# Where the second and third expert's rows stand in the queues of an attention and expert kernel

## The chip, the cores and the metric

The kernel runs on one core of one Trainium2 chip. The metric is the device time of one execution in microseconds (us); several runs are made and their median is compared. The engines have an in-order instruction stream each: TensorE (PE; its weight loads are PEld), VectorE (DVE), ScalarE (ACT), GpSimd (POOL) and SyncE (SP, which only issues transfers here). A tile framework writes the streams: it takes the program's instructions in its order and places each in its engine's queue by its own plan of what is ready when, and it adds the semaphore waits.

## The reference

Three steps, each on the output of the one ahead. The change lies in the second.

```python
# 1. attention: B 2, H 8, S 576, head dim 64; half of the heads local, half strided masks -> x, 1152 x 512
# 2. mixture of experts: E 8, F 1024, capacity 288; one expert for a token
logits = x @ w_gate                      # 512 x 8
expert_idx = argmax(logits, 1); gate_w = softmax(logits)[expert_idx]
disp[e, place in e] = x[token]           # rows of an expert's tokens
h = maximum(disp @ w1, 0)                # 512 -> 1024
y = h @ w2                               # 1024 -> 512
out[token] = gate_w * y[e, place in e]
# 3. feed-forward: h = out @ w_in (512 -> 2048); (h - tanh(h)) @ w_out
```

## The kernel before

All products of the experts and of the feed-forward are made with float16 pairs: a float32 operand is split into a high and a low part (`split`: ScalarE writes the high part, VectorE the low part), and a product is three matmuls, high by high, high by low, low by high (`mm3`). Weights come as float32 in 1 MB halves (`load_w`, tile `st`, four buffers, issued by SyncE) and are split in pieces (`split_w`) into `w1h`, `w1l`, `w2h`, `w2l`. A fifth load into `st` waits until VectorE has split the first.

After attention and routing, the loop over the eight experts `e` runs:
- `gather(e)`: GpSimd fetches the rows of an expert's tokens by index into two tiles `xg` of 96 rows (four buffers, so two experts at a time).
- `tokens(e)`: ScalarE scales `xg` by the gates in place, TensorE transposes it (four small matmuls for a half, out of `xg` with the identity in `iw`), ScalarE and VectorE split the transposed half into `xh` and `xl`.
- `stage1(e)`: the first products, four groups (`fp` 0 to 3) of 24 matmuls of 192 columns; after each group ScalarE applies the relu and writes `hh`, VectorE writes `hl`. Ahead of each group stand some items of `extra`, the splits of weights needed later. The tokens of the next expert (`mid`) are called ahead of group 1.
- `stage2(e - 1)`: the second products of the expert ahead, 96 matmuls with `hh`, `hl` and the second weights; the result goes to `x2h`, `x2l`, in the order of the experts.

`w10`, `w11` and `w20` are loads made early, in attention: first weights of experts 0 and 1, second weights of expert 0. Before, what is left of `w11` (two pieces) and all of `w20` (four) is split in `stage1(0)`. `expert_order` and `token_ids` compute, between the stages, where a token goes; they give small VectorE operations and small products (`ob`, `oa`). `piece` splits a part of `w_in` or `w_out` (tile `raw`, three buffers). `keep_warm` runs matmuls on zeros (`zz`) while the routing is under way. `tc.issue_after(i)` makes an instruction stand behind `i` on the same engine; `behind()` does so for ScalarE and VectorE with their latest instructions.

The profile writes nearly all instructions as line 75, that of the helper that remembers an engine's last instruction; they are told apart by their tiles.

Of the kernel before, what the change touches and what calls it, by code (L numbers as in the profile page):

```python
# [21 lines left out]
E, F1 = 8, 1024  # L22
# [35 lines left out]
BETA = C0 / C2 - ALPHA * ALPHA  # L58
# h - tanh(h) by odd powers of h from the third on
SERIES = [1.0 / 3, -2.0 / 15, 17.0 / 315, -62.0 / 2835, 1382.0 / 155925, -21844.0 / 6081075, 929569.0 / 638512875,  # L60
# [4 lines left out]
class _Last:  # L65
    """An engine that remembers its last instruction."""

# [14 lines left out]
def kernel(  # L82
# [9 lines left out]
    act, dve, pool, pe = _Last(nc.scalar), _Last(nc.vector), _Last(nc.gpsimd), _Last(nc.tensor)  # L92
    sp = nc.sync

    @contextmanager
    def behind():
        # what the block adds on ACT and DVE is issued after what they have so far
        with tc.issue_after(act.last.ins), tc.issue_after(dve.last.ins):
            yield
# [9 lines left out]

# [1 line left out]
    iw = cst.tile([P, NCH, P + E], F32, name="iw")  # L111
# [15 lines left out]

# [1 line left out]
    # sums of the low parts: not finite where a high part is not  # L129
    lsum = cst.tile([P, NLS], F32, name="lsum")  # L130
    lcol = iter(range(NLS))
    pool.memset(lsum, 0.0)

    # sums of squares of a part of each operand, over their least
    sq = cst.tile([P, len(SQ_MIN)], F32, name="sq")
# [24 lines left out]
    def f64_split(hi, lo, raw, scale, n=512):  # L160
        # the bits of -w 2^128 as a float32; sizes from 1 on come out as not finite. A shift by three leaves the two
        # top bits of the exponent set; the last three bits of the fraction are the top ones of the low word
        top = raw.rearrange("p (n two) -> p n two", two=2)[:, :, 1]
        low = raw.bitcast(U16).rearrange("p (n four) -> p n four", four=4)[:, :, 1]
        a = f64p.tile([P, n], U32, tag="fa", name="fa")
        act.activation(a, low, AF.Copy, scale=2.0 ** -13, bias=2.0 ** -14 - 0.5)
        dve.scalar_tensor_tensor(a, top, 3, a, op0=ALU.logical_shift_left, op1=ALU.bitwise_or)
        dve.scalar_tensor_tensor(a, top, 0x80000000, a, op0=ALU.bitwise_and, op1=ALU.bitwise_xor)
        square_once("w_in" if scale == SWI else "w_out", hi, a.bitcast(F32), 2.0 ** -128)
        split(hi, lo, a.bitcast(F32), -scale * 2.0 ** -128, check=True)  # L170
# [26 lines left out]
    def get_w(w, e, n=2):  # L197
        # the halves, and what splits them bit by bit
        lds = [load_w(w, half, e) for half in range(2)]
        return [ld[1:3] for ld in lds], [lambda ld=ld, i=i: split_w(ld, i, n) for ld in lds for i in range(0, NCH, n)]  # L200
# [20 lines left out]

# [1 line left out]
    KT = STRIDE + S + 64  # L223
# [5 lines left out]
    act.activation(warm, warm, AF.Exp)  # L229
    # the clock of the products' array rises while the first rows are on their way  # L230
    zz = cst.tile([P, 512], BF16, name="zz")
# [9 lines left out]
    WARM = (2, 7, 5, 6, 3, 3)  # L241
    # rows past the keys stay zero: the products take all 128 rows
    for t in vts:
# [9 lines left out]
    def load_qk(b, hp, first=False):  # L253
        qt = pa.tile([P, NST * P], F32, tag="q", name="qt")
        kt = pa.tile([P, KT], F32, tag="k", name="kt")
        if first:
            # what the first group of tiles takes goes first
            sp.dma_start(mk[:, :4 * P], masks[:, :4 * P])
# [21 lines left out]

    # the last ones are local: only their last tiles' tokens wait for the end
    pairs = [(0, 0), (0, 1), (0, 2), (0, 3), (1, 2), (1, 3), (1, 0), (1, 1)]
# [82 lines left out]
    def logits_part(first, c, xT, parts, late):  # L365
        # parts: (tile of tokens, where it starts in the sequence)
        lp = bank()
        lv = lp[:, : len(parts) * (P + E)].rearrange("p (t e) -> p t e", e=P + E)
        xw = pa.tile([P, 3, P], F32, tag="xw", name="xw", bufs=4)
        for i, (t, s0) in enumerate(parts):  # L370
            r0, r1 = max(0, -s0), min(P, S - s0)
            pe.matmul(lv[r0:r1, i, :], xT[:, s0 + r0:s0 + r1], iw[:, c, :], start=True, stop=True)
        # whole tiles in one go, a part of a tile by itself
        whole = [k for k, (t, s0) in enumerate(parts) if 0 <= s0 <= S - P]
# [33 lines left out]
    def last_logits(xT, tl, t0):  # L408
        # the routing waits for these: straight onto the other pairs' sums, and the rows of x after them
        c = pairs[-1][1]  # L410
# [31 lines left out]

# [1 line left out]
    def bce(ap, n):  # L444
# [17 lines left out]
    def route(a, b, src):  # L462
        # tokens' experts, ranks and slots; the tiles up to b, after those up to a
        n, ts = b - a, slice(a, b)
# [4 lines left out]
        dve.tensor_tensor(oh[:, ts], bct(desc, n), bce(pm[:, ts], E), op=ALU.is_equal)  # L469
        # ranks in the bank's columns up to 72, tokens of slots in those up to 88, their gates in those past them  # L470
        if a == 0:
# [14 lines left out]
        dve.scalar_tensor_tensor(as_[:, ts], pm[:, ts], -2.0, hf[:, ts], op0=ALU.mult, op1=ALU.add)  # L486
        # the segments' numbers less 2 E, against -2 (E - e) + half
        dve.tensor_tensor(oha[:, ts], bct(seg, n), bce(as_[:, ts], NSEG), op=ALU.is_equal)
# [5 lines left out]
    def gates(a, b):  # L494
        # a slot's gate: the softmax's largest entry, in three exact parts, zero past the capacity
        n, ts = b - a, slice(a, b)
# [84 lines left out]
    def expert_order():  # L581
        # where a token goes in the order of experts, and which token a place there is
        dve.tensor_tensor(lt, bct(desc, NTT), bce(pm, E), op=ALU.is_lt)
# [37 lines left out]

# [1 line left out]
    ffr, ffn = ExitStack(), ExitStack()  # L623
# [9 lines left out]
    def gather(e):  # L633
        # the rows of an expert's tokens
        rows = []
# [7 lines left out]
    def tokens(e, rows):  # L643
        # columns of tokens times their gates
        xh = pm_.tile([P, NCH, SLOT], F16, tag="xh", name="xh")
# [20 lines left out]

    def stage1(xh, xl, whl, extra, mid=None):
        hh = pm_.tile([P, NF1, SLOT], F16, tag="hh", name="hh")
        hl = pm_.tile([P, NF1, SLOT], F16, tag="hl", name="hl")
        for fp in range(NF1 // 2):  # L670
            with behind():
                for x in extra[fp::NF1 // 2]:
                    x()
            if fp == 1 and mid:
                mid()
            hp_ = bank()
            for j in range(2):
# [4 lines left out]
                for c in range(NCH):  # L682
                    mm3(o, wh[:, c, fs], wl[:, c, fs], xh[:, c, :], xl[:, c, :], c == 0, c == NCH - 1)
            hv = hp_[:, : 2 * SLOT].rearrange("p (f k) -> p f k", f=2)
            act.activation(hh[:, 2 * fp:2 * fp + 2, :], hv, AF.Relu)
            dve.scalar_tensor_tensor(hl[:, 2 * fp:2 * fp + 2, :], hv, 0.0, hh[:, 2 * fp:2 * fp + 2, :],
                                     op0=ALU.max, op1=ALU.subtract)
# [20 lines left out]
    with behind(), tc.issue_after(last_x):  # L708
        NB = 6
# [4 lines left out]
    first_gather.append(pool.last.ins)  # L714
    xs[0] = tokens(0, rows)
    rows = gather(1)
    with tc.issue_after(pool.last.ins):
# [7 lines left out]
    for e in range(E):  # L725
        if e > 0:
            w2s[e], ex = get_w(2, e)
            if e == 1:
                for ld in wdma[-2:]:
                    after_gather(ld)  # L730
        else:
            ex = [lambda i=i: split_w(w11[i // 4], i % 4, 1) for i in range(NB, 8)]
            ex += [lambda i=i: split_w(w20[i // 2], i % 2 * 2, 2) for i in range(4)]
            k = -(-len(ex) // 4)
            ex = [ex[j * k + i] if j * k + i < len(ex) else (lambda: None) for i in range(k) for j in range(4)]

        def next_tokens():
            xs[e + 1] = tokens(e + 1, rows)

        hs[e] = stage1(*xs.pop(e), w1s.pop(e), ex, next_tokens if e + 1 < E else None)  # L740
        ex = []
# [27 lines left out]
    ffr.close()  # L769
# [1 line left out]
    pw = ffn.enter_context(tc.tile_pool(name="pw", bufs=1, reuse_waits="tile"))  # L771
# [31 lines left out]
    def ffn2(k, gh, gl):  # L803
# [12 lines left out]
        if k == 0:  # L816
            # the later weights are still on their way: all tokens for a slice of them
            ops = [bank() for _ in range(nj)]
# [12 lines left out]
    def trouble():  # L831
        # on how many partitions what the way above rests on fails: the tokens of an expert fit, the series holds,
        # nothing is past float16's range, and h and a part of each operand are large enough for it
        ok = pw.tile([P, 3 + len(SQ_MIN)], F32, name="ok")
# [20 lines left out]
    def general():  # L855
        # any counts and sizes: all experts for all tokens in float32, weighted by the gate or zero
        with ExitStack() as gx:
# [68 lines left out]
    def tanh_shrink(pool_, hp):  # L926
        # a series up to h^2 = 1/4, past it the difference
        def t(name):
# [34 lines left out]
def _layout(inputs):  # L963
# [6 lines left out]
    a = {}  # L970
    # local heads: pairs of heads; 64 queries against 96 keys
    ql = np.zeros((B, 2, 2, D, NLT, 2, 64), dt)
# [34 lines left out]
    a["w_out"] = np.ascontiguousarray(inputs["moe2_w_out"]).view(np.uint64)  # L1007
    # constants of the shapes alone
    NEG = -1.0e10
# [47 lines left out]
```

## Time and profile before

| | us |
|---|---|
| runs of the kernel before | 434.90, 431.78, 432.42 |
| median of these | 432.42 |
| span of the profiled execution, first to last instruction | 432.6 |
| TensorE busy | 399.6 |
| VectorE busy | 298.4 |
| ScalarE busy | 261.6 |
| GpSimd busy | 39.3 |

The profiled execution is one execution; its own time is not listed beside its span, which lies within the runs' range. Experts run from about 96 to 240 us of the span, the feed-forward from there to the end. Matmuls are pipelined: the starts of two matmuls in a row tell what one costs, the duration written beside it is longer. A granted clock of 1.0 is 2.4 GHz, of 0.5 is 1.2 GHz.

### The profile page before, as it was taken

What the parts mean: (1) busy time and instruction counts of PE and PEld (TensorE: products, weight loads), DVE (VectorE), ACT (ScalarE), POOL (GpSimd) and SP (SyncE); (2) the same over time, 40 slices, a digit from 0 to 9 for tenths busy, and PEclk for the clock granted to TensorE, in tenths of its full rate; (3) what the DMA queues carried; (4) which work ended last, traced back from release to release, by engine and by line L of the source; (5) the groups of instructions that cost most, each with busy time, mean ns of one, the idle gap of its engine ahead of it and who ended that gap; (6) DMA issues with size and microseconds to landing.
All of it is one profiled execution on the core that took longest, in us unless ns stands there. A gap on an engine that the chain in (4) does not pass through costs nothing.

```text
span 432.6 us, 8410 instructions
## 1 busy us (share of the span) xinstructions
PE 399.6 (92%) x3192; PEld 298.5 (69%) x3192; DVE 298.4 (69%) x752; ACT 261.6 (60%) x612; POOL 39.3 (9%) x44
## 2 busy tenths in 40 slices
PE   6699598864999999999999999999999999999994
PEld 3598598723999999999999566665444655444441
DVE  2388589772898979899999799999983678000000
ACT  3377387443996777876974799899752887100000
POOL 6000000066102011000000000000000100000000
PEclk9699699995999999999999999999999999999998
DMA  8797488626879788789724423312350100000000
GB/s 217 218 295 230 152 269 236 213 93 205 291 262 354 279 291 302 243 302 341 259 101 148 147 97 113 131 59 89 99 194 17 58 1 2 24 27 27 24 26 27
DMA packets 33514, 69.92 MB, mean 162 GB/s; under 512 B 3108, under 2 KB 9252, under 8 KB 33468
## 3 DMA queue, kind: packets, MB, share of 16 engines
q1 hardware_dynamic: 31580, 63.68, 44.7%
q0 software_dynamic: 1744, 5.51, 3.8%
q8 instruction: 27, 0.44, 0.4%
q14 instruction: 19, 0.16, 0.1%
q10 hardware_dynamic: 144, 0.13, 0.1%
HBM read 64.59 MB, written 4.72 MB: 160 GB/s over the span
## 4 chain that ended last, share of the span: by engine, by line
PE 42%; DVE 9%; issue 8%; DMA 3%; ACT 2%; POOL 0%; POOLq 0%; DVEq 0%; ACTq 0%
PE bank L75 42%; DVE w2l L75 3%; DMA xg<-xd,ids 2%; DVE w1l L75 2%; DVE fa L75 2%; DVE hl L75 1%; ACT w2h L75 1%; DMA out_dram<-ob,ids 1%; ACT win_h L75 1%; DVE x2l L75 0%; DVE xl L75 0%; DVE win_l L75 0%; ACT x2h L75 0%; POOL xg L75 0%; POOL out_dram L75 0%
## 5 line engine op out<-in xcount | busy, mean ns | idle before, releaser
L75 PE MATMUL bank<-xh,w1h 128*128 128x192 f16 x256 | 64.0, 250 | 7.6 <-ACT xh L75 7.6
L75 PE MATMUL bank<-xh,w1l 128*128 128x192 f16 x256 | 64.1, 250 | 0.7 <-DVE w1l L75 0.5
L75 PE MATMUL bank<-xl,w1h 128*128 128x192 f16 x256 | 64.0, 250 | 0.0
L75 PE MATMUL bank<-x2l,win_h 128*128 128x384 f16 x192 | 62.6, 326 | 0.5 <-DVE ok L75 0.5
L75 PE MATMUL bank<-hl,w2h 128*128 128x192 f16 x256 | 63.0, 246 | 0.0
L75 PE MATMUL bank<-hh,w2h 128*128 128x192 f16 x256 | 63.0, 246 | 0.0
L75 PE MATMUL bank<-hh,w2l 128*128 128x192 f16 x256 | 63.0, 246 | 0.0
L75 PE MATMUL bank<-x2h,win_h 128*128 128x384 f16 x192 | 62.6, 326 | 0.0
L75 PE MATMUL bank<-x2h,win_l 128*128 128x384 f16 x192 | 62.6, 326 | 0.0
L75 PEld LDWEIGHTS <-win_h 128*128 128x128 f16 x384 | 37.6, 98 | 25.8 <-DVE ok L75 0.7
L75 PE MATMUL bank<-wo_h,gh 128*128 128x512 f16 x144 | 54.6, 379 | 0.0
L75 PE MATMUL bank<-wo_l,gh 128*128 128x512 f16 x144 | 54.6, 379 | 0.0
L75 PE MATMUL bank<-wo_h,gl 128*128 128x512 f16 x144 | 54.6, 379 | 0.0
L75 PEld LDWEIGHTS <-gh 128*128 128x128 f16 x288 | 28.1, 98 | 33.6
L75 PEld LDWEIGHTS <-w1h 128*128 128x128 f16 x512 | 47.2, 100 | 0.3
L75 PEld LDWEIGHTS <-w2h 128*128 128x128 f16 x512 | 46.1, 98 | 0.0
L75 DVE SCALAR_TENSOR_TENSOR fa<-raw,fa 128x512 uint32<-128x512 uint32 x64 | 42.8, 684 | 2.1 <-ACT fa L75 1.7
L75 ACT ACTIVATE ob<-bank 128x512 f32<-128x512 f32 x9 | 5.4, 597 | 62.6 <-PE bank L75 60.1
L75 DVE SCALAR_TENSOR_TENSOR w2l<-st,w2h 128x1024 f16<-128x1024 f32 x32 | 38.8, 1217 | 2.9 <-ACT w2h L75 2.6
L75 DVE SCALAR_TENSOR_TENSOR w1l<-st,w1h 128x1024 f16<-128x1024 f32 (+1 forms) x40 | 38.4, 1003 | 0.3 <-ACT w1h L75 0.2
L75 DVE SCALAR_TENSOR_TENSOR w<-z,y 128x384 f32<-128x384 f32 x48 | 26.0, 552 | 15.2 <-ACT z L75 15.2
L75 PE MATMUL bank<-kt,qt 128*108 128x108 f32 (+2 forms) x160 | 23.5, 292 | 12.1 <-DMA kt<-in_k_str_dram 5.7
(144 smaller groups left out, 765.5 us busy)
## 6 DMA issues: line engine op xcount, KB each, us to landing
st<-in_w_dram SPq DMA_DIRECT2D x32, 1024.0 KB, 5.8
raw<-in_w_in_dram SPq DMA_DIRECT2D x16, 512.0 KB, 5.6
raw<-in_w_out_dram SPq DMA_DIRECT2D x16, 512.0 KB, 3.5
qt<-in_q_str_dram SPq DMA_DIRECT2D x4, 594.0 KB, 6.0
xd<-xw SPq DMA_DIRECT2D x15, 128.0 KB, 2.0
vt<-in_v_loc_dram SPq DMA_DIRECT2D x4, 432.0 KB, 6.1
qt<-in_q_loc_dram SPq DMA_DIRECT2D x3, 576.0 KB, 9.0
kt<-in_k_str_dram SPq DMA_DIRECT2D x4, 297.0 KB, 6.7
```

Source lines behind the costliest of these rows:

```text
L75: self.last = f(*a, **k)
```

## The change

The tokens of expert 1 are called ahead of group 3 of `stage1(0)` instead of group 1, those of expert 2 ahead of group 2 of `stage1(1)` (`mid_at` is 3 - e for the first two experts, else 1). Their instructions stand behind the matmuls so far on TensorE, and on ScalarE behind the relu of group 1 (for expert 1) or group 0 (for expert 2). The splits of `w20` move from `stage1(0)` to `stage1(1)`, where they share the eight places with the splits of expert 1's own second weights; of the two pieces left of `w11` both come ahead of group 0. Comments also go, which only moves line numbers.

```diff
-    def stage1(xh, xl, whl, extra, mid=None):
+    def stage1(xh, xl, whl, extra, mid=None, mid_at=1):
...
-            if fp == 1 and mid:
-                mid()
+            if fp == mid_at and mid:
+                with tc.issue_after(pe.last.ins) if fp > 1 else nullcontext():
+                    mid()
...
             act.activation(hh[:, 2 * fp:2 * fp + 2, :], hv, AF.Relu)
+            relus[fp] = act.last.ins
...
             if e == 1:
+                ex = w20s[::2] + ex[::2] + w20s[1::2] + ex[1::2]
                 for ld in wdma[-2:]:
                     after_gather(ld)
         else:
-            ex = [lambda i=i: split_w(w11[i // 4], i % 4, 1) for i in range(NB, 8)]
-            ex += [lambda i=i: split_w(w20[i // 2], i % 2 * 2, 2) for i in range(4)]
-            k = -(-len(ex) // 4)
-            ex = [ex[j * k + i] if j * k + i < len(ex) else (lambda: None) for i in range(k) for j in range(4)]
+
+            left = [lambda i=i: split_w(w11[i // 4], i % 4, 1) for i in range(NB, 8)]
+            w20s = [lambda i=i: split_w(w20[i // 2], i % 2 * 2, 2) for i in range(4)]
+            none = lambda: None
+            ex = [left[0], none, none, none, left[1]]
 
         def next_tokens():
-            xs[e + 1] = tokens(e + 1, rows)
-
-        hs[e] = stage1(*xs.pop(e), w1s.pop(e), ex, next_tokens if e + 1 < E else None)
+
+            with tc.issue_after(relus[1 - e]) if e < 2 else nullcontext():
+                xs[e + 1] = tokens(e + 1, rows)
+
+        hs[e] = stage1(*xs.pop(e), w1s.pop(e), ex, next_tokens if e + 1 < E else None, 3 - e if e < 2 else 1)
```

ScalarE, from the scaling of expert 0's rows on (`xg<-xg,gsl`: two for each expert), before:

```order
L75 ACTIVATE xg<-xg,gsl 96x512 [waits DMASW0_49,DVE_49]
L75 ACTIVATE xg<-xg,gsl 96x512 [waits DMAHW5_49,DMAHW6_49,DMAHW4_49,DMASW1_49]
L75 ACTIVATE xh<-bank 128x4x96 [waits PE_49]
L75 ACTIVATE xg<-xg,gsl 96x512 [waits DMAHW7_49,DMASW2_49]
L75 ACTIVATE xh<-bank 128x4x96 [waits PE_49]
L75 ACTIVATE w1h<-st 128x512 x2
L75 ACTIVATE xh,sq<-bank 128x4x96 [waits PE_49]
```

The same place after the change:

```order
L75 ACTIVATE xg<-xg,gsl 96x512 [waits DMASW0_49,DVE_49]
L75 ACTIVATE xg<-xg,gsl 96x512 [waits DMAHW5_49,DMAHW6_49,DMAHW4_49,DMASW1_49]
L75 ACTIVATE xh<-bank 128x4x96 [waits PE_49] x2
L75 ACTIVATE w1h<-st 128x512 x2
L75 ACTIVATE hh<-bank 128x384 [waits PE_49] x2
L75 ACTIVATE xg<-xg,gsl 96x512 [waits DMAHW7_49,DMASW2_49]
L75 ACTIVATE xg<-xg,gsl 96x512 [waits DMAHW0_49,DMASW3_49]
```

The first scaling of expert 1 stood between the two `xh` of expert 0; now both scalings of expert 1 stand behind two relus of expert 0.

ScalarE in the groups of expert 0 and 1, before, from expert 0's first relu on (`xg` rows: experts 2 and 3):

```order
L75 ACTIVATE hh<-bank 128x384 [waits PE_49]
L75 ACTIVATE w2h,sq<-st 128x512
L75 ACTIVATE w2h<-st 128x1024
L75 ACTIVATE w2h<-st 128x1024 [waits Activation_49]
L75 ACTIVATE xh<-bank 128x4x96 [waits PE_49]
L75 ACTIVATE hh<-bank 128x384 [waits PE_49]
L75 ACTIVATE w2h<-st 128x1024 x2
L75 ACTIVATE hh<-bank 128x384 [waits PE_49]
L75 ACTIVATE xg<-xg,gsl 96x512 [waits DMASW4_49]
L75 ACTIVATE xg<-xg,gsl 96x512 [waits DMASW5_49]
```

After, from the relu of expert 0's last group on to the scalings of expert 2:

```order
L75 ACTIVATE hh<-bank 128x384 [waits PE_49]
L75 ACTIVATE w2h,sq<-st 128x512
L75 ACTIVATE w2h<-st 128x1024 [waits Activation_49]
L75 ACTIVATE w2h<-st 128x1024
L75 ACTIVATE hh<-bank 128x384 [waits PE_49]
L75 ACTIVATE w2h<-st 128x1024 x2
L75 ACTIVATE hh<-bank 128x384 [waits PE_49]
L75 ACTIVATE w2h<-st 128x1024 [waits DMAHW1_49]
L75 ACTIVATE w2h<-st 128x1024
L75 ACTIVATE xg<-xg,gsl 96x512 [waits DMASW4_49]
L75 ACTIVATE xg<-xg,gsl 96x512 [waits DMASW5_49]
```

Six `w2h` and a square now stand between expert 0's last relu and the scalings of expert 2. Right behind them, after the change, the scalings of experts 3 and 4 follow, ahead of the relu of expert 1's third group:

```order
L75 ACTIVATE xg<-xg,gsl 96x512 [waits DMASW6_49]
L75 ACTIVATE xh<-bank 128x4x96 [waits DVE_49,PE_49]
L75 ACTIVATE xg<-xg,gsl 96x512 [waits DMASW7_49]
L75 ACTIVATE xh<-bank 128x4x96 [waits PE_49]
L75 ACTIVATE xg<-xg,gsl 96x512 [waits DMASW0_49,Activation_49]
L75 ACTIVATE xg<-xg,gsl 96x512 [waits DMASW1_49,Activation_49]
L75 ACTIVATE hh<-bank 128x384 [waits PE_49]
L75 ACTIVATE w2h<-st 128x1024 [waits DMAHW3_49]
```

The last two `xg` rows are expert 4's; before, they stood behind the first `x2h` of expert 0's second products. On TensorE the eight transposes of expert 1 stood after 1 and after 24 products of expert 0 and now stand after 72; those of expert 2 stood after 24 products of expert 1 and now stand after 48. The GpSimd queue has the same rows in the same order.

## Rows read from the trace of the kernel before

**Rows 1.** Stage table: window, length, busy (x instructions) of PE, PEld, DVE, ACT, POOL; clock, DMA share, GB/s.
```profile
148.20:164.70 16.50, 16.50 (x202) 16.50 (x201) 13.34 (x25) 11.71 (x18) 1.85 (x2) 1.00 0.77 267
```
**Rows 2.** Waits of TensorE, whole span: us in total, times, longest.
```profile
PE bank L75 <- ACT xh L75: 7.6, 1, 7.6
...
PE bank L75 <- DVE ok L75: 0.5, 1, 0.5
PE bank L75 <- DVE w1l L75: 0.5, 1, 0.5
```
**Rows 3.** ScalarE in order of time: start, us, instruction, idle before and its releaser.
```profile
94.13 0.72 ACT L75 ACTIVATE xg<-xg,gsl 96x512 f32<-96x512 f32 x1 [0.88 <-DMA xg<-xd,ids]
...
102.51 0.72 ACT L75 ACTIVATE xg<-xg,gsl 96x512 f32<-96x512 f32 x1 [7.29 <-DMA xg<-xd,ids]
103.14 0.47 ACT L75 ACTIVATE xh<-bank 128x384 f16<-128x384 f32 x1
```
**Rows 4.** TensorE in order of time, at the points that the sum uses.
```profile
47.99 1.75 PE L75 MATMUL bank<-kt,qt 128*108 128x108 f32 x8 [5.66 <-DMA kt<-in_k_str_dram]
...
95.29 0.81 PE L75 MATMUL bank<-zz 128*128 128x512 bf16 x3
103.66 0.32 PE L75 MATMUL bank<-xh,w1h 128*128 128x192 f16 x1 [7.56 <-ACT xh L75]
...
114.96 0.24 PE L75 MATMUL bank<-xh,w1h 128*128 128x192 f16 x1
...
116.94 0.83 PE L75 MATMUL bank<-iw,xg 96*128 96x96 f32 x8
...
123.78 0.24 PE L75 MATMUL bank<-hh,w2h 128*128 128x192 f16 x1
...
131.69 0.25 PE L75 MATMUL bank<-xh,w1h 128*128 128x192 f16 x1
```
**Rows 5.** Stage table by single microseconds; the third number from the end is the clock.
```profile
44.00:45.00 1.00, 0.00 (x0) 0.00 (x0) 1.00 (x5) 0.59 (x2) 0.00 (x0) 0.70 1.03 334
...
51.00:52.00 1.00, 1.00 (x10) 1.00 (x10) 0.00 (x0) 1.00 (x6) 0.00 (x0) 0.89 0.05 22
...
99.00:100.00 1.00, 0.00 (x0) 0.00 (x0) 0.00 (x0) 0.00 (x0) 1.00 (x2) 0.51 1.06 408
...
109.00:110.00 1.00, 1.00 (x13) 0.97 (x12) 0.49 (x1) 1.00 (x3) 0.29 (x1) 0.87 0.95 336
```
**Rows 6.** ScalarE in order of time, splits, a relu and two scalings.
```profile
109.33 1.99 ACT L75 ACTIVATE w2h<-st 128x1024 f16<-128x1024 f32 x2
...
113.86 0.50 ACT L75 ACTIVATE hh<-bank 128x384 f16<-128x384 f32 x1
114.23 1.34 ACT L75 ACTIVATE xg<-xg,gsl 96x512 f32<-96x512 f32 x2
```
**Rows 7.** VectorE in order of time, order sums and splits.
```profile
116.83 0.17 DVE L75 COPY off<-bank 128x16 f32<-128x16 f32 x1
...
120.29 1.22 DVE L75 SCALAR_TENSOR_TENSOR w2l<-st,w2h 128x1024 f16<-128x1024 f32 x1
...
128.86 1.21 DVE L75 SCALAR_TENSOR_TENSOR w1l<-st,w1h 128x1024 f16<-128x1024 f32 x1
```
**Rows 8.** GpSimd and SyncE in order of time, then the gathers' landing times.
```profile
96.39 0.92 POOL L75 DMA_INDIRECT xg<-xd,ids  x1 [0.30 <-PE bank L75]
...
118.19 0.91 POOL L75 DMA_INDIRECT xg<-xd,ids  x1 [7.57 <-ACT xg L75]
...
105.50 0.37 SPq L186 DMA_DIRECT2D st<-in_w_dram  x1
...
DMA to landing us min/median/max: 3.1/6.0/10.4
```
**Rows 9.** DMA queues, 97 to 99 us, then 100 to 102 (q1 SyncE, q0 GpSimd): packets, MB, share.
```profile
q1 hardware_dynamic: 332, 0.72, 99.1%
...
q0 software_dynamic: 109, 0.32, 50.0%
```

More of the change, by code (lines that the diff above doesn't have):

```diff
@@ L715 @@
     xs[0] = tokens(0, rows)
+    relus = {}
     rows = gather(1)
```

## The prediction

> **What bounds the kernel now.** I read the times by stage first. In a whole expert stage TensorE is busy for all of its 16.50 us while VectorE works 13.34 and ScalarE 11.71 [rows 1]: from the experts on, the matmul queue sets the pace. Then the waits of TensorE: after the routing there is one long one, 7.6 us before a product of expert 0, released by ScalarE's xh, and two of 0.5 us [rows 2]. So what is gained up to some point of the expert stages reaches the end, unless a supplier (ScalarE, VectorE, a gather) then comes too late.
>
> ScalarE's own rows say why it waits. It scales the second half of expert 0's rows at 94.13, and its next row is a scaling for expert 1, at 102.51, after the gather landed; only behind it comes the xh of 103.14, the second half of expert 0's columns [rows 3]. The queue is in order, so expert 0 waits for expert 1's rows. TensorE's last keep-warm product ends at 95.29 + 0.81 = 96.1, its first expert product starts at 103.66 [rows 4]. The clock's share falls to 0.51 in the microsecond from 99 and is back only in that from 109 [rows 5], so the stall also makes the first 5.5 us of work run at half clock (1.2 instead of 2.4 GHz): 7.6 + some 2.7 us, about 10.2 in all, are lost. First products of expert 1 start at 114.96, those of expert 2 at 131.69 [rows 4]. The sum follows these two points.
>
> **The change, step by step.** The profiled span is 432.6 us, 0.2 above the median of 432.42; I apply the difference of the sum to the median.
>
> Expert 0 starts on time. In the new ScalarE order nothing stands between expert 0's two scalings and its two xh. The second half's four transposes end near 95.5, xh takes 0.47 [rows 3]: 96.0, and xl follows on VectorE near 96.6. The start moves from 103.66 to 96.1, with the array still warm. A product costs 7.91 / 96 = 0.0824 us (96 second products from 123.78 to 131.69) [rows 4]. The 72 products that now precede expert 1's transposes end at 96.6 + 69 x 0.0824 = 102.3.
>
> Expert 1's rows. Their gather landed at 102.5 [rows 3]; 0.72 of scaling, the second half 0.62 behind, and four transposes each (0.83 for eight [rows 4]) end at 104.4, so TensorE waits some 1.5 us. One thing could make them later. The two VectorE splits left over for expert 1 end near 98 instead of 105.4, and these free the buffer for the 1 MB load that SyncE issued at 105.50 [rows 8]; it and two loads of w_in (0.5 MB each; in the new order a third one comes ahead of the next weights) go out near 98, while expert 1's gathers, the second of them issued at 96.39 [rows 8], are in flight. From 97 to 99 SyncE's queue moved 0.72 MB and the gathers nothing, from 100 to 102 the gathers moved 0.32 MB [rows 9]: they moved when what had been issued before them was through. If order of issue decides, the new loads stand behind the gathers and cost nothing; if SyncE's queue goes first, 2 MB at 0.36 MB/us cost 5.5 us. The rows fit the first; I take 1 us and keep 0 to 5.5. Transposes end at 105.4, 24 products later, at 107.4, expert 1 starts, against 114.96: 7.6 ahead.
>
> Expert 2's rows behind the splits. The four splits of w20 now come in the first two of expert 1's four groups of products, and two splits of its own also stand ahead of the scalings. So in ScalarE's new queue six long w2h rows and one square lie between the last relu of expert 0 and expert 2's scalings. From 107.4: relu 0.38, square 0.6, then two w2h, relu, two w2h, relu, two w2h, scaling. A w2h costs 1.99 / 2, pipelined 0.95; relu 0.37; two scalings 1.34 [rows 6]. That is 0.38 + 0.6 + 3 x 1.9 + 2 x 0.37 + 0.72 = 8.1: the first half is ready at 115.6, the second at 116.2, the transposes end at 116.8. TensorE has only 48 products, 4.0 us, until it needs them: it stands still from 111.4 to 115.6. Before, these transposes came after 24 products and ended at 117.77; 24 more products make that 119.6, so 2.8 us are left of the 7.6. This is the price of the moved splits; before, they lay in the time of expert 0, beside slow products.
>
> Clock. Two waits show what 4.2 us of standing still may do. In the 5.66 us before 47.99 the clock fell in the microsecond from 44, some 2 us in, and was back in that from 51, 3.2 us after work resumed; in the 7.56 us before 103.66 it fell 2.9 us in and came back after 5.5 us of work [rows 4, 5]. At half clock 3.2 to 5.5 us of work lose 1.6 to 2.75; if it falls only as work resumes, or not at all, less. I take 1.4, ends 0 and 2.75. The other 48 products (4.0), the small products for the tokens' places (0.24) and expert 0's 96 second products (7.9) then end at 116.8 + 12.1 + 1.4 = 130.3.
>
> VectorE must have the second weights of expert 0 by then: from 107.5 the order sums (116.83 to 120.29, 3.5 us), a low part of 0.47, four w2l of 1.14 [rows 7] and one more 0.47 end at 116.5, needed from 121 on: covered.
>
> ScalarE's next knot. In the new order the scalings of experts 3 and 4, four rows, stand ahead of the relu of expert 1's third group. Expert 4's gather takes the buffers that expert 2's transposes leave; before, GpSimd began it at 118.19, 1.25 us after those transposes began at 116.94 [rows 4, 8]. Now: 116.9 and 1.2 later, and 6.0 us to landing (median; 3.1 to 10.4) [rows 8]: 124.2 for the second half, scaled at 124.9. Until then ScalarE is stuck. Behind it stand relu, two w2h, relu, then w1h of expert 2, at 127.5; on VectorE hl, two w2l, hl, then the w1l of expert 2 (1.15 each [rows 7]): 130.15 for the first, 131.3 for the second, which TensorE needs 0.5 us into expert 2. That lets expert 2 start, in effect, at 130.8. Both paths, 130.3 and 130.8, end close together; the later one decides: 131.69 - 130.8 = 0.9 us gained. With 0 instead of 1 us at expert 1's rows, the fast landing and no loss of clock it is 131.69 - 127.9 = 3.8; with the slow ends it is negative.
>
> After that the order differs little, and VectorE has 3 us to spare per stage [rows 1], so I carry 0.9 to the end: 432.4 - 0.9 = 431.5 us. The added waits (issue_after) are order of issue on one engine and cost nothing by themselves; the GpSimd queue has the same rows in the same order.
>
> **Rivals.**
> Kept: expert 2's rows don't hold TensorE up, and most of the 10.2 us stays. For it: the stall removed is real, and TensorE has hardly any other. Against: 8.1 us of ScalarE rows against 4.0 us of products is not close. It needs ScalarE's queue to stand otherwise than the order shows; time 422 to 428.
> Neutral: the lead at expert 2 is eaten further on. The wait of 0.5 us for w1l [rows 2] shows that weights come just in time; loads, gathers, scaling, splits form a ring of their own, and if it turns no earlier, TensorE meets it two experts on. Against: VectorE's 3 us of slack and gathers that follow TensorE's transposes. Time 432 to 433.
> Slower: the gathers are held back twice, expert 1's behind the 2 MB that now start at 98, expert 4's behind the loads for expert 2. It decides from 2 us of delay at expert 1 on, since then TensorE stands still for 3.5 us there too and loses the clock a second time, or from a landing of 7 us at expert 4: 131.69 is passed by 1 to 5 us. Time 433.5 to 438. For it: the one landing of 10.4 us. Against: gathers so far moved by order of issue.
> Turns: gathers and loads share the DMA engines, so that neither the 2 MB at 98 nor any backlog holds a gather up. The 1 us falls away, expert 4's rows land nearer to the 3.1 us than to the 6.0, and TensorE's own path decides: 130.3 - 1.0 = 129.3, 2.4 us gained, 430.0; without a loss of clock 428.6. For it: landings of 3.1 us occur. Against: two microseconds with 0.72 MB in SyncE's queue and no gather packet, though the gather of 96.39 was on its way [rows 8, 9].
> The Trainium skill states this rule: "DMA: Bandwidth & Descriptors", Queues, rings and completion order, says that each DMA engine takes turns between the queues that have work, a packet at a time. On these rows the trace does not agree with it.
>
> **How the numbers follow.** Forecast (430.5 to 432) 0.40, turns (428 to 430.5) 0.22, neutral 0.14, slower 0.16, kept 0.08. About 1%, 4.3 us, is what a measurement of this kernel can tell from no change: 428.1 and 436.7. Faster by more: kept and the lower edge of turns, 0.14; slower by more: the upper part of its rival, 0.10; within 1%: 0.76. The range leaves out kept and the worst of slower: 428.0 to 434.9.
>
> **What the profile after would show.** Right: no wait before expert 0's first product, at 96.1, with the clock share at 1.0 through 110; a wait of 1 to 3 us for xg before expert 1's transposes near 102; a wait of about 4 us, released by ScalarE's xg, before expert 2's transposes near 111 to 116; a clock share of 0.5 for some microseconds behind it; ScalarE idle for the gather of expert 4 at 117 to 124; expert 2's first products at 130 to 131. Wrong: no wait near 111 (then kept), or the expert-1 wait above 4 us (then slower). If expert 2 starts near 130 but the last experts no earlier than before, it is neutral.

## The result and the profile after

The changed kernel takes 436.28 us (median of six runs, 434.77 to 439.95) against 432.28 before: ratio 1.0101, 95% interval 1.0063 to 1.0139. It is about 1% slower; I had forecast 431.5, and the time lies above the range of 428.0 to 434.9. The medians in this document are over all runs, while the ratios leave out four runs that lie more than 1.5% above the fastest of their kernel, one each of hold and tokens_only and two of gather_first, and the profiles of tokens_only and gather_first are of such runs.

The profiled execution is the longest of the six (439.95, span 438.2). Attention, which the change doesn't touch, ended 1.08 us earlier in it than in the trace of before, so I count from the end of the last keep-warm product: 95.29 + 0.81 = 96.10 before [rows 4], 94.21 + 0.81 = 95.02 after. TensorE in order of time after the change (start, us, instruction, idle before and its releaser):

```profile
94.21 0.81 PE L75 MATMUL bank<-zz 128*128 128x512 bf16 x3
94.95 0.41 PE L75 MATMUL bank<-xh,w1h 128*128 128x192 f16 x3
...
102.37 0.55 PE L75 MATMUL bank<-iw,xg 96*128 96x96 f32 x4 [0.97 <-ACT xg L75]
103.46 0.55 PE L75 MATMUL bank<-iw,xg 96*128 96x96 f32 x4 [0.55 <-ACT xg L75]
105.86 0.24 PE L75 MATMUL bank<-xh,w1h 128*128 128x192 f16 x1
...
114.37 1.29 PE L75 MATMUL bank<-iw,xg 96*128 96x96 f32 x8 [4.39 <-ACT xg L75]
...
129.78 0.26 PE L75 MATMUL bank<-xh,w1h 128*128 128x192 f16 x1 [0.49 <-ACT w1h L75]
131.59 0.26 PE L75 MATMUL bank<-xh,w1l 128*128 128x192 f16 x1 [1.47 <-DVE w1l L75]
132.73 0.34 PE L75 MATMUL bank<-xh,w1l 128*128 128x192 f16 x1 [0.48 <-DVE w1l L75]
...
244.65 0.34 PE L75 MATMUL bank<-x2h,win_h 128*128 128x384 f16 x1
```

The 7.6 us ahead of expert 0 [rows 2, 4] are gone. In their place stand 1.5 us for expert 1's rows and 4.39 for expert 2's. Expert 2 starts 34.76 us after the last keep-warm product; before it was 131.69 - 96.10 = 35.59, so at that point 0.83 us were gained. The loss comes behind it. Here are the first-product stages of experts 2 to 6, each from its first product to the first second product behind it (window, length, then busy time of PE, PEld, DVE, ACT, POOL; clock third from the end), after:

```profile
129.78:142.11 12.33, 10.38 (x104) 9.80 (x105) 11.03 (x21) 9.41 (x16) 1.84 (x2) 0.86 0.91 317
150.05:160.68 10.63, 8.95 (x107) 8.49 (x106) 9.75 (x18) 7.60 (x12) 1.94 (x2) 1.00 0.95 304
168.60:178.35 9.75, 8.93 (x107) 8.48 (x106) 8.87 (x17) 6.72 (x12) 1.94 (x2) 1.00 1.01 346
186.27:196.28 10.01, 8.93 (x107) 8.48 (x106) 9.13 (x17) 6.97 (x12) 0.00 (x0) 1.00 0.98 348
204.20:212.78 8.58, 8.58 (x106) 8.58 (x105) 7.70 (x13) 4.54 (x10) 0.00 (x0) 1.00 1.02 378
```

and the stages of experts 2, 4 and 5 before, and, in order of time, the first product of the feed-forward before:

```profile
131.69:140.28 8.59, 8.59 (x108) 8.59 (x106) 7.33 (x16) 6.20 (x11) 2.43 (x2) 1.00 0.96 352
...
164.70:173.61 8.91, 8.76 (x107) 8.54 (x106) 8.03 (x15) 5.87 (x11) 1.94 (x2) 1.00 1.03 368
181.53:190.99 9.46, 8.93 (x106) 8.48 (x105) 8.58 (x17) 6.43 (x11) 0.00 (x0) 1.00 0.99 351
```

```profile
239.36 0.34 PE L75 MATMUL bank<-x2h,win_h 128*128 128x384 f16 x1
```

A stage without a wait takes 8.58. Expert 2 lost 12.33 - 8.59 = 3.74 (2.44 of waits; the rest at half clock), expert 3 2.05, expert 4 0.84, expert 5 0.55 more than before. Less the 0.83 gained that is 6.35; from keep-warm to feed-forward it went from 143.26 to 149.63, which is 6.37. (The medians differ by 4.0; this is the longest run.) In this execution the waits of TensorE for w1l were 5.5 us in all, 0.5 before [rows 2].

Why w1l comes late is read from ScalarE, VectorE and GpSimd, each in order of time:

```profile
113.60 1.94 ACT L75 ACTIVATE xg<-xg,gsl 96x512 f32<-96x512 f32 x3
...
115.81 0.72 ACT L75 ACTIVATE xg<-xg,gsl 96x512 f32<-96x512 f32 x1
116.43 0.48 ACT L75 ACTIVATE xh<-bank 128x384 f16<-128x384 f32 x1
124.80 1.33 ACT L75 ACTIVATE xg<-xg,gsl 96x512 f32<-96x512 f32 x2 [7.90 <-DMA xg<-xd,ids]
126.04 0.47 ACT L75 ACTIVATE hh<-bank 128x384 f16<-128x384 f32 x1
...
115.35 2.35 DVE L75 SCALAR_TENSOR_TENSOR w2l<-st,w2h 128x1024 f16<-128x1024 f32 x2
...
118.57 0.09 DVE L75 DVE_READ_ACCUMULATOR xl<-bank,xh 128x1 f32 x1
126.54 0.56 DVE L75 SCALAR_TENSOR_TENSOR hl<-bank,hh 128x384 f16<-128x384 f32 x1 [7.89 <-ACT hh L75]
...
130.31 1.22 DVE L75 SCALAR_TENSOR_TENSOR w1l<-st,w1h 128x1024 f16<-128x1024 f32 x1
...
115.67 2.82 POOL L75 DMA_INDIRECT xg<-xd,ids  x1 [9.84 <-PE bank L75]
118.80 0.92 POOL L75 DMA_INDIRECT xg<-xd,ids  x1 [0.30 <-issue]
```

ScalarE has expert 4's scalings (124.80) ahead of a relu of expert 1 that is ready long before. It stands 7.90 us for the gather, VectorE stands 7.89 behind it, and w1l of expert 2 begins at 130.31, when its products have already begun. Two things stood in the gather's way. GpSimd's issue took 2.82 us instead of 0.92 [rows 8] and ended at 118.49, 0.79 us after VectorE's two `w2l` (115.35 + 2.35). And by then SyncE's queue had been given three 1 MB loads since 112.26, the last at 117.73; the queues from 116 to 122, and then from 122 to 124 us (packets, MB, share):

```profile
q1 hardware_dynamic: 1076, 2.14, 102.7%
...
q0 software_dynamic: 113, 0.36, 67.6%
q1 hardware_dynamic: 128, 0.23, 33.0%
```

No gather packet moved until the loads were nearly through. From the start of that issue to the first scaling it took 124.80 - 115.67 = 9.13 us.

### The profile page after: what moved, and what is told of

It is laid out like the page before. It is cut to its first block, busy times and chain, and to the rows that moved or that the text cites. A ratio compares the mean times of both kernels' runs of the same rounds, so it can differ in the third digit from the quotient of the medians.

```text
span 438.2 us, 8408 instructions
## 1 busy us (share of the span) xinstructions
PE 402.5 (92%) x3192; PEld 299.1 (68%) x3192; DVE 298.4 (68%) x752; ACT 262.1 (60%) x612; POOL 40.7 (9%) x44
## 4 chain that ended last, share of the span: by engine, by line
PE 42%; DVE 9%; issue 8%; DMA 4%; ACT 3%; POOL 0%; POOLq 0%; ACTq 0%; DVEq 0%
PE bank L75 42%; DMA xg<-xd,ids 4%; DVE w2l L75 3%; DVE w1l L75 2%; DVE fa L75 2%; DVE hl L75 1%; ACT w2h L75 1%; DMA out_dram<-ob,ids 1%; ACT win_h L75 1%; DVE x2l L75 0%; DVE xl L75 0%; DVE win_l L75 0%; ACT x2h L75 0%; ACT hh L75 0%; POOL out_dram L75 0%
## 5 line engine op out<-in xcount | busy, mean ns | idle before, releaser
L75 PEld LDWEIGHTS <-win_h 128*128 128x128 f16 x384 | 37.6, 98 | 25.8 <-DVE ok L75 0.7
L75 ACT ACTIVATE w2h<-st 128x1024 f16<-128x1024 f32 (+1 forms) x33 | 34.1, 1044 | 0.0
```

Of the source, the lines that this page charges most:

```text
L75: self.last = f(*a, **k)
```

## The experiments

Theory K (knot): the time is lost because expert 4's scalings stand in ScalarE's queue ahead of work for experts 1 and 2, and the lateness is handed on. Rival S (splits): it is lost through the moved splits of `w20`, by the 4.39 us and by later loads into their buffers. The times below are medians, and ratios against the kernel before on the same chip with 95% intervals; the chips differ from run to run. Counted from the end of keep-warm, as above, the profiled executions show (us):

| kernel | expert 2 starts | feed-forward starts |
|---|---|---|
| before | 35.59 | 143.26 |
| changed | 34.76 | 149.63 |
| changed, once more | 35.46 | 148.19 |
| hold | 36.71 | 142.99 |
| hold4 | 36.69 | 144.14 |
| tokens_only | 37.61 | 147.31 |
| tokens_hold | 31.30 | 137.58 |
| tokens_knot4 | 31.72 | 141.77 |
| splits_only | 36.43 | 151.50 |
| gather_first | 34.95 | 145.66 |
| gap | 36.87 | 146.20 |
| hold_before | 35.84 | 142.12 |
| mid3_hold | 32.95 | 139.23 |
| e1_hold | 34.42 | 140.70 |

**hold**: the scalings of expert k (from 3 on) stand behind the last relu of expert k - 2 (`lastr` collects those).

```diff
-            with tc.issue_after(relus[1 - e]) if e < 2 else nullcontext():
+            with tc.issue_after(relus[1 - e] if e < 2 else lastr[e - 1]):
```

> The changed kernel, with the scalings of expert k's rows (k from 3 on) queued behind the last relu of expert k - 2, so that expert 4's scalings no longer stand ahead of expert 1's last two relus. Theory K (the knot: ScalarE stands 7.9 us for expert 4's gather with expert 1's relus, second and expert 2's first weights behind it, and the ring of splits, loads and gathers stays late): ScalarE doesn't stand still there, the 2.4 us of waits for w1h and w1l at expert 2 and the half clock behind them go (2.4 + some 1.3), and so do most of the 1.7, 0.8 and 1.1 us at experts 3 to 5: 429 to 431.5 us, faster than the kernel before by 0.2 to 0.8%. The waits for xg ahead of expert 1's and expert 2's transposes (1.5 and 4.4 us) stay. Rival S (the moved splits are what costs, by the 4.4 us and by the later loads into their buffers): the w1l waits at experts 2 and 3 stay or come back as waits for w1h because the loads were issued late: 434 to 436 us.

430.56 us, ratio 0.9941 (0.9909 to 0.9972): faster than before where the changed kernel is slower. The waits for the rows of experts 1 and 2 stay (1.86 and 4.04 us), and the clock is at half from 114.1 to 120.9, as the clock's column has it (0.56 in the microsecond from 114, 0.53 in that from 120), but no stage behind it waits at all. TensorE's row, and expert 2's stage in the table by stage:

```profile
115.07 1.54 PE L75 MATMUL bank<-iw,xg 96*128 96x96 f32 x8 [4.04 <-ACT xg L75]
```

```profile
130.72:139.31 8.59, 8.59 (x107) 8.59 (x106) 7.18 (x14) 7.41 (x13) 3.22 (x2) 1.00 0.85 279
```

K holds: 5.7 us between the two medians come from the place of these scalings alone.

**hold4**: only expert 4's scalings held (`if e < 2 or e == 3`, behind the last relu of expert 2).

> The changed kernel, with only expert 4's scalings held (behind the last relu of expert 2); those of experts 3 and 5 to 7 stand where the change put them. Theory R (one late gather is enough, and the ring of loads, splits and gathers passes the lateness on): no wait at expert 2 and none of over 0.5 us for w1l at experts 3 to 5, as with all of them held: 429.5 to 431.5 us. Rival O (every stage has its own knot, since each expert's scalings stand ahead of relus): the waits for w1l at experts 3 to 5 stay at 0.5 to 1.7 us each: 432 to 434 us.

431.80 us, 0.9988 (0.9955 to 1.002), which lies between the two forecasts, 0.3 us above theory R's. The waits are as R has them: expert 2 has none, expert 3 none; experts 4 and 5 have 0.27 and 0.39 us. So it is in the main one knot, not one for each expert: with the first gone, of the 1.69, 0.82 and 1.08 us for w1l at experts 3 to 5 in the changed kernel 0, 0.27 and 0.39 are left. Holding the other scalings too gives another 1.2 us (430.56, intervals overlapping).

**tokens_knot4**: the reverse, in the fastest version (tokens_hold below): expert 4's scalings alone let go (`if e != 3`).

> The fastest version so far (splits back in the first stage, scalings from expert 3 on held), with one thing undone: expert 4's two scalings are not held and stand again ahead of expert 1's last two relus; all the others stay held. Theory K (these two rows are the knot, wherever the splits stand): ScalarE stands there for expert 4's gather for 4 to 7 us, w1l comes late at expert 2, TensorE waits 1 to 3 us there and 0.5 to 1.5 us at expert 3: 429 to 432 us. Rival (without the moved splits the gather lands in time, the two rows cost nothing): 426 to 427.5 us.

433.63 us on a chip where the kernel before took 435.74: 0.9943 (0.9899 to 0.9988), against 0.9848 with these two rows held, about 4 us. GpSimd, SyncE, ScalarE and TensorE in order of time, then expert 2's stage in the table by stage:

```profile
117.76 1.01 POOL L75 DMA_INDIRECT xg<-xd,ids  x1 [7.11 <-PE bank L75]
...
117.99 12.26 SPq L186 DMA_DIRECT2D st<-in_w_dram  x2
...
125.30 0.72 ACT L75 ACTIVATE xg<-xg,gsl 96x512 f32<-96x512 f32 x1 [7.16 <-DMA xg<-xd,ids]
...
131.60 0.26 PE L75 MATMUL bank<-xh,w1l 128*128 128x192 f16 x1 [1.28 <-DVE w1l L75]
132.75 0.26 PE L75 MATMUL bank<-xh,w1l 128*128 128x192 f16 x1 [0.48 <-DVE w1l L75]
```

```profile
129.98:142.33 12.35, 10.59 (x104) 10.02 (x105) 10.71 (x20) 10.44 (x18) 2.09 (x2) 0.86 0.93 324
```

Expert 2's stage is back at 12.35 us (12.33 in the changed kernel), without any moved split. It is back without a long issue on GpSimd, too: the first took 1.01 us, a 1 MB load (the first of the two in SyncE's row) went out at 117.99 while it was under way, and ScalarE's scaling came 125.30 - 117.76 = 7.54 us after the start of the issue. Expert 3 had no wait, though 0.5 to 1.5 us were expected: with the later scalings held, the lateness isn't handed on.

**tokens_only** and **splits_only**: half of the change each. In the first the lines that build `ex` for experts 0 and 1 are those of before; in the second the tokens are called at group 1 and unheld, as before.

> Half of the change: the later place of experts 1's and 2's tokens, with the splits of expert 0's second weights back in the first stage. Theory K: expert 4's scalings still stand ahead of expert 1's last two relus, so ScalarE still stands there for 6 to 8 us, but some 2 to 3 us earlier, since expert 2's rows come at about 112 instead of 114; a wait of 0.5 to 2 us for w1l at expert 2 stays: 430 to 433 us. Rival S (the splits): all of the loss goes: no wait of over 1.5 us ahead of expert 2's transposes, no half clock, no wait for w1l at experts 2 to 5: 425 to 429 us.

> The other half of the change: the splits of expert 0's second weights a stage later, with the tokens called as in the kernel before. The 7.6 us wait ahead of expert 0 stays. Theory K: expert 4's scalings don't stand ahead of expert 1's relus in this order, so little is lost: 432 to 434 us. Rival S: the loads of expert 2's first weights go out later, since their buffers come free with the moved splits, and TensorE waits for w1h or w1l at expert 2 for 2 us and more: 434 to 438 us.

tokens_only: 435.85 us, 1.0056 (1.0022 to 1.009), above both ranges. The splits' return gained almost nothing. The plan now tied two knots, one for expert 2's first gather ahead of expert 0's last relu, one for expert 4's (in other profiles, e1_hold has a stand of 3.81 us for the first of these gathers, tokens_knot4 one of 7.16 for the second); ScalarE:

```profile
114.09 0.72 ACT L75 ACTIVATE xg<-xg,gsl 96x512 f32<-96x512 f32 x1 [6.50 <-DMA xg<-xd,ids]
114.72 0.47 ACT L75 ACTIVATE hh<-bank 128x384 f16<-128x384 f32 x1
...
127.95 1.33 ACT L75 ACTIVATE xg<-xg,gsl 96x512 f32<-96x512 f32 x2 [6.45 <-DMA xg<-xd,ids]
129.19 0.47 ACT L75 ACTIVATE hh<-bank 128x384 f16<-128x384 f32 x1
```

splits_only: 442.04 us, 1.019 (1.012 to 1.0259), worse than both ranges. It keeps the stall ahead of expert 0 (8.2 us). As rival S said, the loads for expert 2 went out late (123.14 us against 112.26 in the changed kernel), and ScalarE waited 0.93 us for one; but TensorE's waits at expert 2 are 0.4 us, not the 2 and more of rival S, and the longest wait, 3.5 us for w1l at expert 3, stands behind scalings of expert 5 that ScalarE met ahead of a relu of expert 2 (2.39 us for the gather). So the run doesn't part K from S; it shows the splits cost something by themselves.

**tokens_hold**: tokens_only with the hold of all scalings.

> Both of these edits: the splits of expert 0's second weights back in the first stage, and the scalings from expert 3 on behind the last relu of expert k - 2. Theory K and rival S agree that it is the fastest: no long wait at expert 2, no knot. Of the 7.6 us and the half clock ahead of expert 0 (10.2 in all) the 1.5 us for expert 1's rows remain and up to 4 us at expert 2: 424 to 428 us. If it is at 431 or above, what limits lies elsewhere (loads or gathers).

426.86 us, 0.9848 (0.9803 to 0.9893): faster than both kernels, and the best here. Against hold, 3.7 us come from the splits' old place. TensorE waits 2.54 and 2.13 us for the rows of experts 1 and 2, the clock stays at 1.0, and expert 2 starts 4.3 us earlier than before, all of which reaches the feed-forward (5.7).

**hold_before**: the hold alone, in the kernel before.

> The kernel before, with the scalings from expert 3 on behind the last relu of expert k - 2, and nothing else changed. Theory K: these scalings hold nothing up in the kernel before but the waits of 0.3 and 0.5 us for w1l at experts 4 and 5, so at most 0.8 us is gained: 431.3 to 432.5 us. Rival H (holding them is a gain of its own in any order, and says nothing on the change): 428 to 430 us.

429.47 us, 0.9931 (0.9891 to 0.997). Theory K's number was wrong and rival H's right: the hold is a gain of its own. In the traces it takes 1.1 us off the stretch to the feed-forward, which are the 0.33 and 0.88 us by which the stages of experts 4 and 5 before exceed 8.58; where the rest of the 2.8 us lies, these single executions don't show. H doesn't explain the loss: the hold is worth 2.8 us in the kernel before and 5.7 in the changed one, and with it in both the change is neither gain nor loss (429.47 and 430.56, intervals overlapping).

**gather_first**: expert 4's gather is called ahead of `get_w(2, 2)`, whose two loads wait for it.

```diff
+            if e == 2:
+                rows4 = gather(4)
             w2s[e], ex = get_w(2, e)
+            if e == 2:
+                for ld in wdma[-2:]:
+                    tc.add_manual_dep(ld.ins, pool.last.ins.name, ...
```

> The changed kernel, with the two loads of expert 2's second weights issued only behind GpSimd's gather of expert 4's rows (before, one of them went out between the two gathers). ScalarE's order is the same. If transfers move in the order of issue, the rows land some 2.7 us earlier, by 122 instead of 124.7, ScalarE stands 5 instead of 7.9 us, the waits for w1l at expert 2 fall from 2.4 to under 0.5 us: 433 to 435 us. If what is queued on SyncE's queue goes ahead of a gather that was issued earlier, the load of 1 MB still overtakes it, the rows land no more than 1 us earlier, and ScalarE still stands 7 to 8 us: 435.5 to 437 us.

433.84 us, 1.0038 (1.0005 to 1.0071). The load waited for the landing, not for the issue (it went out at 125.67), so this can't tell the order of transfers. It does show the price of the load: the first issue was still long (2.47 us), but ScalarE stood 3.96 + 0.71 us instead of 7.90, its first scaling came 124.25 - 119.42 = 4.83 us after the start of the issue, expert 2 had no wait for w1l, and 2.4 us of the median came back. Expert 3's 1.04 + 0.48 and later waits stayed. GpSimd and ScalarE in order of time:

```profile
119.42 2.47 POOL L75 DMA_INDIRECT xg<-xd,ids  x1 [10.25 <-ACT xh L75]
...
124.25 0.72 ACT L75 ACTIVATE xg<-xg,gsl 96x512 f32<-96x512 f32 x1 [3.96 <-DMA xg<-xd,ids]
```

**gap**: on VectorE two `w2l` stand behind the two `xl` of expert 2, and no other queue's order is changed.

```diff
+                ex[2::4] = [lambda x=x: high_only(x) for x in ex[2::4]]
...
                     mid()
+                with tc.issue_after(dve.last.ins):
+                    while lows:
+                        lows.pop(0)()
```

> The changed kernel with one swap on VectorE: the two low parts of expert 0's second weights that ran while GpSimd issued expert 4's first gather now stand behind the two low parts of expert 2's columns. The other engines' orders are the same. In the changed kernel GpSimd's issue took 2.82 us there, and ended within 0.2 us of the end of VectorE's unbroken run; elsewhere such an issue takes 0.92. Theory V (VectorE's split with two operands from SBUF keeps GpSimd from issuing): the first issue takes 0.9 to 1.3 us, both gathers are out before the next 1 MB load of second weights, expert 4's rows land 2 to 4 us earlier, ScalarE stands 4 to 6 instead of 7.9 us, the waits for w1l at expert 2 fall below 1 us: 432 to 434.5 us. Rival (the issue's length has another cause, such as the transfers queued ahead): it stays at 2.4 to 2.9 us, ScalarE stands 7 to 8 us: 436 to 437 us.

433.59 us, 0.9999 (0.9962 to 1.0035). GpSimd, VectorE and ScalarE in order of time, then expert 2's stage:

```profile
117.78 0.92 POOL L75 DMA_INDIRECT xg<-xd,ids  x1 [11.21 <-PE bank L75]
119.00 0.92 POOL L75 DMA_INDIRECT xg<-xd,ids  x1 [0.31 <-ACT xh L75]
...
119.17 2.35 DVE L75 SCALAR_TENSOR_TENSOR w2l<-st,w2h 128x1024 f16<-128x1024 f32 x2
...
122.98 1.33 ACT L75 ACTIVATE xg<-xg,gsl 96x512 f32<-96x512 f32 x2 [4.33 <-DMA xg<-xd,ids]
```

```profile
131.58:140.16 8.58, 8.58 (x106) 8.58 (x105) 7.28 (x14) 5.77 (x12) 1.84 (x2) 1.00 1.04 368
```

Theory V holds in all of its numbers but one. The issue takes 0.92, both gathers are out before the next load (121.60), ScalarE stands 4.33 us, and expert 2's stage has no wait; but expert 4's rows are there 28.3 us after keep-warm instead of 29.8, which is 1.5 us earlier and not 2 to 4. The run changes two things at once: that load waits for a buffer that these two `w2l` free, so it goes out later too (121.60; 117.73 in the changed kernel). The first scaling comes 122.98 - 117.78 = 5.20 us after the start of the issue. Small waits at experts 3 to 5 stay (2.0 us in all), for ScalarE is still 4 us late with expert 1.

**changed_again**: the changed kernel as it is.

> The changed kernel as it is, once more, since its profiled execution was the longest of its six runs (439.95 against a median of 436.28). Theory K: a more usual execution has the same order of things, ScalarE standing 5 to 8 us for expert 4's gather, w1l late at experts 2 to 5, with the waits of TensorE there adding up to 3 to 6 us; 435 to 437 us. If the waits at experts 2 to 5 are under 1.5 us in all and the time is the same, theory K explains only the longest run.

436.85 us, 1.0102 (1.0041 to 1.0164). ScalarE stands 7.83 us for expert 4's rows, GpSimd's issue takes 2.47, and TensorE waits 2.36 us at expert 2 and 0.70, 0.41 and 0.64 at experts 3 to 5. The order of things is the same, the later waits smaller than in the longest run. GpSimd, then ScalarE:

```profile
115.19 2.47 POOL L75 DMA_INDIRECT xg<-xd,ids  x1 [11.09 <-PE bank L75]
...
123.88 1.34 ACT L75 ACTIVATE xg<-xg,gsl 96x512 f32<-96x512 f32 x2 [7.83 <-DMA xg<-xd,ids]
```

**mid3_hold** (tokens_hold with expert 2's tokens ahead of group 3) and **e1_hold** (with them at group 1, unmoved):

> The version with the splits back in the first stage and the scalings from expert 3 on held, and expert 2's tokens called ahead of group 3 instead of group 2 of expert 1's products: 72 products, 6 us, instead of 48 cover expert 2's rows, but one more long split stands ahead of their scalings. If the wait was only for a fixed queue, the 2.1 us shrink to under 0.7: 424.5 to 426 us. If the scalings move back as far as the transposes, a wait of 1 to 2 us stays: 426 to 427.5 us.

> Expert 1's tokens late as in the changed kernel, expert 2's tokens called where the kernel before has them, splits in the first stage as before, scalings from expert 3 on held. Of the waits in the fastest version 2.5 us ahead of expert 1's transposes stay, those of 2.1 us ahead of expert 2's should shrink, since two long splits fewer stand ahead of their first scaling: 425 to 427 us. If expert 2's scalings come no earlier, TensorE waits there with 24 instead of 48 products ahead, up to 4 us: 428 to 430 us.

428.16 us, 0.9891 (0.9843 to 0.994), and 430.64 us where before took 435.74, 0.988 (0.9845 to 0.9915). Both lie above both of their forecasts, and neither beats 0.9848. In mid3_hold the scalings moved back as far as the transposes and the wait stayed at 2.13 us; in e1_hold ScalarE stood 3.81 us for expert 2's first gather, and TensorE waited 1.69 us for xh of expert 1 behind it.

## Why the prediction was wrong

Right, step by step: expert 0 on time, with 0.20 us of wait; 1.5 us for expert 1's rows (0.97 + 0.55), without the extra 1 us; expert 1's start 10.84 us after keep-warm (11.3 forecast); 4.39 us for expert 2's rows (4.2 forecast); the end of expert 0's second products 34.3 us after keep-warm (34.2 forecast). The clock was at half for 3.4 us behind that wait; the stretch from 105.86 to 121.21 took 15.35 us against 8.82 before, which leaves 2.1 us beside the 4.39 (1.4 taken, 0 to 2.75 kept). That the 2 MB from 98 on would not hold expert 1's gathers up was right too.

Wrong: **ScalarE's next knot**, which I saw and priced too low. I had w1l of expert 2 ready at 130.15 and 131.3, 34.05 and 35.2 us after keep-warm; the two pieces ended at 131.45 and 132.59 (36.4 and 37.6), 2.4 us later. In the terms of the sum: the second gather was to begin 1.2 us after the first and the rows to land 6.0 us later, so that 7.3 us lay between the start of the first issue (116.9) and the scaling (124.2); measured were 9.13, which is 1.8 of the 2.4. The other 0.6 is a second scaling that I had counted as hidden. The two gathers' median landing was 7.6 us, not 6.0 (6.2 in changed_again, where the first scaling still came 8.69 us after the start of the issue). My rival Slower, which has expert 4's gather behind the loads for expert 2, named 7 us there as the point from which it decides, and its 433.5 to 438 holds the result; its other place, expert 1's rows, had no delay. I gave it 0.16, for want of a reason why the gather should be slower there.

What the term left out is the load. Where a 1 MB load goes out while the first issue is under way, the first scaling comes 9.13 us after the start of that issue (changed kernel, issue 2.82), 8.69 (changed_again, 2.47), 7.54 (tokens_knot4, 1.01) and 6.86 (tokens_only, 1.06); where none does, 4.83 (gather_first, 2.47) and 5.20 (gap, 0.92). So late rows go with the load's place, and a long issue without such a load doesn't bring them. That the change puts `w2l` splits on VectorE just where GpSimd issues I hadn't seen either; I had taken the 1.2 us from a place where VectorE ran no long split [rows 8]. Whether a short issue alone would have brought both gathers ahead of the load at 117.73 no run shows, since gap, 2.7 us faster than the changed kernel, moved that load too.

Wrong as well: **I carry 0.9 to the end**. That expert 2's first product came 0.83 us earlier than before looks like the forecast 0.9, but is luck: the 0.9 had the wait for w1l in it, and with it expert 2's stage ended 2.9 us later than before, counted from keep-warm. Expert 3 lost 2.05 us more, experts 4 and 5 another 1.4 together, against slack of 3 us per stage on VectorE [rows 1]. A ring hands the delay on: late w1l frees `st` late, so the next loads go out late (expert 3's at 132.71, 37.7 us after keep-warm, against 130.11 and 34.0 before), stand ahead of expert 5's gather, and ScalarE stands 3.09 us at 145.48 for it with expert 2's relu behind. hold4 and tokens_knot4 show both conditions: it needs the first delay and the later scalings ahead of the relus. Average slack doesn't help an engine that stands in order behind a transfer.

The rival Turns is not borne out: from 116 to 122 us SyncE's queue moved 2.14 MB and the gathers nothing, though the first was issued by 118.49. The Trainium skill, "DMA: Bandwidth & Descriptors", Queues, rings and completion order, has each DMA engine take turns between the queues that it has work for. On these rows the trace again does not agree; order of issue fits. It isn't so clean everywhere: in tokens_knot4, where a load was issued at 108.51 and gathers at 108.50 and 109.73, SyncE's queue moved 0.80 MB and the gathers 0.42 in the same four microseconds from 112 on.

One slip in the working changes no sum: 24 more products behind 117.77 end at 119.75, not 119.6, so 2.95 us instead of 2.8 were left of the 7.6.

Of the two parts of the change, with the knots untied, the later tokens gain 2.6 us (429.47 in hold_before, 426.86 in tokens_hold) and the moved splits lose 3.7 (430.56 in hold).

## What to carry to other kernels

When code is moved, read the whole new queue of each in-order engine, also two stages on: the costly rows here were scalings that the diff doesn't mention, put by the plan ahead of relus whose inputs were ready. Hold work that waits for a transfer behind work that feeds the next stage, even where it seems free (here 0.7%, in a kernel whose stages showed 1.2 us above 8.58). And take a gather's price from a place where the neighbours, the loads queued ahead above all, do what they will do in the new order.

## What the runs showed of the hardware

A gather's issue on GpSimd that begins while VectorE splits weights with both operands in SBUF (`w1l`, `w2l`) ends about 0.8 us after such a split has ended. In the changed kernel that was the second of two (`w2l` to 117.70; issue of 2.82 us, to 118.49). In the trace of before, for expert 1's first gather, it was the last of six (`w1l` to 95.29; issue of 4.00 us from 92.08, to 96.08); no run moved that one. In gap, where the two `w2l` were moved, the issue took 0.92. It isn't always the whole run of splits: in tokens_only an issue of 1.29 us from 104.77 ended 0.79 us after the first of two `w2l` (104.05 to 106.40), and what decides that no run here shows.

The Trainium skill, "SBUF — State Buffer", SBUF: two separate sides, says that VectorE and GpSimd share one pair of ports as an exclusive lock, held for a whole instruction, and that a VectorE operation with two SBUF inputs takes it only against a GpSimd operation that reads SBUF. The trace agrees if a gather's issue, which takes its row numbers from the tile `ids`, counts as such an operation; no run here varies that.
